# Value products over whole key tiles, flat loads for the bounds, and the softmax constant from a column: one change to an attention and two-layer MLP kernel

## The chip, the cores and the metric

The kernel runs on one core of a Trainium2 chip. The metric is the device time of one execution in microseconds (us); of several executions the median is taken. Beside the time there is one profiled execution, and its span is the time from its first to its last instruction.

The engines are named as the profile names them: PE is TensorE (matmuls), PEld its weight loads, DVE is VectorE, ACT is ScalarE, POOL is GpSimd, and SP issues the DMAs.

## The reference

Causal attention with a decay, then two dense layers. There are 4 batches, 8 heads, 576 positions and 64 columns a head; the inputs are float32.

```python
scores = q @ k^T / 8
cum = cumsum(log(clip(f, 1e-4, 1)))
scores = where(causal, -1e9, scores + cum[:, None] - cum[None, :])
attn = exp(scores - max); attn = attn / (sum(attn) + 1e-9)
x = (attn @ v), heads side by side: 2304 x 512
h = x @ w_in (512 x 2048); x = (h * tanh(softplus(h))) @ w_out (2048 x 512)
h = x @ w2_in (512 x 1024); solu = h * softmax(h)
out = (layer norm of solu * g_ln) @ w2_out (1024 x 512)
```

## The kernel before

**Precision.** PE works on float16. Each float32 operand is split into a high and a low float16 part after a scaling by a power of two, and each product is three matmuls: high by high, high by low, low by high. The scale of k and v of a batch comes from a bound on their size: `stats` (line 290) sums squares along rows on ACT, one column for each chunk, and `scales` (line 314) takes the largest column and sums over the partitions.

**Attention.** A batch is cut into five tiles of key or query rows (`rows_of`, line 75). In batch 0 tile 4 holds only rows 0 to 63; in batches 1 to 3 tile 0 holds only rows 64 to 127, and all others are whole. For each query tile i a slot handles four heads (i = 0), two (i = 1) or one (i of 2 to 4):

- `step_s` makes the scores; the matmuls of line 418 contract 128 rows, those of line 419 contract 67.
- `step_r` (line 452) takes the maximum on DVE and the exponential on ACT. It writes the float32 probabilities into one of two tiles `p32`, which are set to zero once at the start, and the sums of rows into `rsum`.
- `step_h` (line 484) splits them into float16 (`ph`), and one DMA transposes them to `pT`, with the keys on the partitions.
- `step_pv` (line 515) makes the value products, for each head and each key tile c up to i three matmuls of 64 columns (lines 537 to 539). The rows that they contract are the valid rows of key tile c, so they are 64 for the half tile and 128 for every other tile.
- `fin` (line 541), once for each query tile, adds 1e-9 to the sums (line 549; the last tile first adds its two partial sums, line 548), takes the reciprocal, scales the product and transposes it into `xT`, from which the first dense layer reads.

**Loads.** k and v of a batch are read twice: once early for the bounds and once when they are split. `ahead` (line 625) does both for the next batch during query tiles 2 to 4. Both readings use `load_raw` (line 274), which reads 64 float32 of a head at a time, so each packet has 256 bytes. All raw tiles share one rotation of three buffers.

**Dense layers.** `up` (line 764) and `down` (line 808) are the matmuls of the first, with ACT, DVE and POOL between them; `Stage2` (lines 1430 and 1470) is the second, which can start its weights only when attention's memory is free.

**Order.** The class `Order` takes all instructions with their dependences, works out a duration for each, simulates them several times and pins the order of the instructions of every engine that ended earliest. Its duration of a matmul (`weigh`, line 1120) is made from the columns alone:

```python
c = elems(next(b for t, b, w in acc if w)) / 2.4
o.cols += c
o.d += max(c + 2.5, 28.0)
```

The functions that the change touches are these.

Of the kernel before, what the change touches and what calls it, by code (L numbers as in the profile page):

```python
# [9 lines left out]
F32 = mybir.dt.float32  # L10
# [181 lines left out]
def emit(tc, q, k, v, f, w_in, w_out, w2_in, w2_out, g_ln, out):  # L192
# [94 lines left out]
            )  # L287
        return i

    def stats(b, c, which):  # L290

        if ("st", b) not in sc:
            sc["st", b] = att.tile([P, 2, NCH], F32, tag="st", name=f"st_{b}", bufs=2)
            nc.vector.memset(sc["st", b], 0.0)
        r0, r1_, _ = rows_of(b, c)
        for nm in which:
            jk = attd.tile([P, DM], F32, tag="x32", name=f"jk{nm}_{b}_{c}", bufs=1)
            nc.scalar.activation(
                jk[r0:r1_], raw[nm, b, c][r0:r1_], AF.Square,
                accum_out=sc["st", b][r0:r1_, "kv".index(nm), c:c + 1])  # L300
# [64 lines left out]
    def split_v(b, c):  # L365
        r0, r1_, _ = rows_of(b, c)
        vc = attd.tile([P, 2, DM], F16, tag="vt", name=f"vt_{b}_{c}", bufs=6)
        vt[b, c] = vc
        rv = raw["v", b, c][r0:r1_]
        s = sc["v", b][r0:r1_]  # L370
        split(nc, vc[r0:r1_, 0], vc[r0:r1_, 1], rv, s, qmode(b, c, 1))
# [80 lines left out]
    def step_r(b, i, hs):  # L452
        m, off, end, sp, wd = pend.pop(("s", b, i, hs))
        if (b, i) not in pend:
            pend[b, i] = attd.tile([P, 2, H], F32, tag="rsum", name=f"rsum_{b}_{i}", bufs=2)
        rs = pend[b, i]
        ng = len(hs)
        nm = attd.tile([P, 4], F32, tag="nm", name=f"nm_{b}_{i}_{hs[0]}", bufs=2)
        pt = p32[cnt["p32"] % len(p32)]
        cnt["p32"] += 1  # L460
        pv = pt.rearrange("p c s -> p (c s)")
        pend["p", b, i, hs] = (m, pt)
        if i < NCH - 1:
            s3 = sp[:m, :wd * ng].rearrange("p (g s) -> p g s", g=ng)
            nc.vector.tensor_reduce(nm[:m, :ng], s3[:, :, off:end], axis=AX.X, op=ALU.max, negate=True)  # L465
            for g, h in enumerate(hs):
                nc.scalar.activation(  # L467
                    pv[:m, g * (i + 1) * P + off:g * (i + 1) * P + end], s3[:, g, off:end],
                    AF.Exp, bias=nm[:m, g:g + 1], accum_out=rs[:m, 0, h:h + 1])
            return  # L470
        h = hs[0]
        ex = sps[2][:m].rearrange("p (h s) -> p h s", h=H)
        if h == 0:
            ne = attd.tile([P, H], F32, tag="ne", name=f"ne_{b}", bufs=1)
            nc.vector.tensor_reduce(ne[:m], ex, axis=AX.X, op=ALU.max, negate=True)
            pend["ne", b] = ne
        ne = pend["ne", b]
        nc.vector.tensor_reduce(nm[:m, 0:1], sp[:m], axis=AX.X, op=ALU.max, negate=True)
        nc.vector.tensor_tensor(nm[:m, 0:1], nm[:m, 0:1], ne[:m, h:h + 1], op=ALU.min)
        x0, m0 = (off, 128) if off else (512, 0)  # L480
        nc.scalar.activation(pv[:m, x0:x0 + 64], ex[:, h], AF.Exp, bias=nm[:m, 0:1], accum_out=rs[:m, 1, h:h + 1])
        nc.scalar.activation(pv[:m, m0:m0 + 512], sp[:m], AF.Exp, bias=nm[:m, 0:1], accum_out=rs[:m, 0, h:h + 1])  # L482
# [32 lines left out]
    def step_pv(b, i, hs):  # L515
        if len(hs) == 1:
            if hs[0] % 2 == 0:
                return
            hs = (hs[0] - 1, hs[0])
        r0, r1_, _ = rows_of(b, i)  # L520
        m = r1_ - r0
        pT = pend.pop(("pT", b, i, hs[0]))
        if hs[0] == 0:
            if pv0 and i == 1:
                pend["pv", b, i] = pv0.pop().tile([P, DM], F32, tag="x2_0", name=f"pv_{b}_{i}")
            else:
                pend["pv", b, i] = pspv.tile([P, DM], F32, tag="pv", name=f"pv_{b}_{i}")
        acc = pend["pv", b, i]
        for g, h in enumerate(hs):
            o = acc[:m, h * D:(h + 1) * D]  # L530
            for c in range(i + 1):
                a0, a1, _ = rows_of(b, c)
                vc = vt[b, c]
                vh = vc[a0:a1, 0, h * D:(h + 1) * D]
                vl = vc[a0:a1, 1, h * D:(h + 1) * D]
                k = 2 * (g * (i + 1) + c)
                nc.tensor.matmul(o, pT[a0:a1, k, :m], vh, start=(c == 0), stop=False)  # L537
                nc.tensor.matmul(o, pT[a0:a1, k, :m], vl, start=False, stop=False)  # L538
                nc.tensor.matmul(o, pT[a0:a1, k + 1, :m], vh, start=False, stop=(c == i))  # L539

    def fin(b, i):
# [2 lines left out]
        rs = pend.pop((b, i))  # L544
        acc = pend.pop(("pv", b, i))
        rr = attd.tile([P, H], F32, tag="rr", name=f"rr_{b}_{i}", bufs=2)
        if i == NCH - 1:
            nc.vector.tensor_tensor(rs[:m, 0], rs[:m, 0], rs[:m, 1], op=ALU.add)
        nc.vector.tensor_scalar(rr[:m], rs[:m, 0], 1e-9, None, op0=ALU.add)
        nc.vector.reciprocal(rr[:m], rr[:m])  # L550
        x32 = attd.tile([P, DM], F32, tag="x32", name=f"x32_{b}_{i}", bufs=1)
        nc.vector.tensor_tensor(
# [72 lines left out]
    def ahead(b, i, h):  # L625

        nb, ni = (b, i + 1) if i + 1 < NCH else (b + 1, 0)
        if b + 1 < B and i in (2, 3, 4):
            n = (i - 2) * H + h
            if n in (6, 8, 14, 15, 16):  # L630
                load_raw(b + 1, (6, 8, 14, 15, 16).index(n), "kv")
            if n in (8, 10, 15, 16, 17):
                stats(b + 1, (8, 10, 15, 16, 17).index(n), "kv")
            if n == 18:
                scales(b + 1, "kv")
        if nb < B:
            if h == (LD if ni else 3) and nb > 0:
                load_raw(nb, ni, "qkv")
            if h == LD and nb == 0 and ni >= 3:
                load_raw(nb, ni, "q")  # L640
            if h == (LD + 2 if ni else 4):
                if nb or ni > 1:
                    split_k(nb, ni)
                    split_q(nb, ni)
                split_v(nb, ni)
# [307 lines left out]
EARLY = {"PE": 0.0, "ACT": 103.0, "DVE": 79.0, "POOL": 37.0, "SP": -45.0}  # L953
LATE = {"PE": 53.0, "ACT": 34.0, "DVE": 33.0, "POOL": 77.0, "SP": 27.0}
HEAD = 126.0
PERIOD = 3413.33
BACKLOG = 1500.0
LANDED = 600.0
# [20 lines left out]
class Order:  # L979
# [140 lines left out]
    def weigh(self):  # L1120

        for o in self.ops:
            if o.eng == "PE":
                for i, acc in o.ins:
                    c = elems(next(b for t, b, w in acc if w)) / 2.4
                    o.cols += c
                    o.d += max(c + 2.5, 28.0)
                    if size_of(next(t for t, b, w in acc if not w).dtype) == 4:
                        o.d += 200.0
# [72 lines left out]
    def plan(self, rank):  # L1202
# [8 lines left out]
        free["SP"] = free["-"] = 0.0  # L1211
        seq = {e: [] for e in engs}
        state = {"lock": 0.0, "dma": 0.0, "end": 0.0}
        busy, warm, win = {}, False, 0
        self.start = start = [0.0] * len(ops)

        def give(o, t):
# [9 lines left out]
        while todo:  # L1227
# [35 lines left out]
            elif e == "PE":  # L1263
# [5 lines left out]
                while todo_c > 1e-6:  # L1269
# [6 lines left out]
                    if todo_c > 1e-6:  # L1276
                        warm = busy[win] / PERIOD >= (0.38 if warm else 0.85)
                        win += 1
                end = t + o.d + x - t - o.cols
                seen = end + 165  # L1280
            elif o.lock:
                end = seen = max(t + HEAD, state["lock"]) + max(o.d - HEAD, 20.0)
# [239 lines left out]
```

## Time and profile before

| | us |
|---|---|
| median of 3 runs | 811.48 (811.48 to 812.52) |
| the profiled execution | 813.11 |
| its span | 811.3 |

| engine | busy, us | share of the span |
|---|---|---|
| PE | 729.6 | 90% |
| DVE | 603.1 | 74% |
| ACT | 546.6 | 67% |
| POOL | 404.3 | 50% |

The profile shows one execution. Busy times are unions of instruction times; matmuls are pipelined, so the listed time of one matmul is longer than its step, and the step is read from the starts of neighbours in the timeline. A row of the timeline merges neighbours of one kind and gives their start, the time from the first start to the last end, and their count. Idle time of an engine costs something only where that engine sets the end.

### The profile page before, as it was taken

What the parts mean: (1) busy time and instruction counts of PE and PEld (TensorE: products, weight loads), DVE (VectorE), ACT (ScalarE), POOL (GpSimd) and SP (SyncE); (2) the same over time, 40 slices, a digit from 0 to 9 for tenths busy, and PEclk for the clock granted to TensorE, in tenths of its full rate; (3) what the DMA queues carried; (4) which work ended last, traced back from release to release, by engine and by line L of the source; (5) the groups of instructions that cost most, each with busy time, mean ns of one, the idle gap of its engine ahead of it and who ended that gap; (6) DMA issues with size and microseconds to landing.
All of it is one profiled execution on the core that took longest, in us unless ns stands there. A gap on an engine that the chain in (4) does not pass through costs nothing.

```text
span 811.3 us, 15742 instructions
## 1 busy us (share of the span) xinstructions
PE 729.6 (90%) x5822; PEld 457.6 (56%) x5822; DVE 603.1 (74%) x1168; ACT 546.6 (67%) x1201; POOL 404.3 (50%) x321
## 2 busy tenths in 40 slices
PE   0345568799999999999999999999999999999998
PEld 0233336476666767676677767665565554444443
DVE  4799998878788887869988966687877437355651
ACT  4464649968996979798986776798694544233332
POOL 2153246766685775675878773247473312112221
PEclk9975659899999999999999999999999999999999
DMA  8999998778987999877997652732313422534543
GB/s 210 246 246 235 256 201 166 142 130 150 172 148 151 188 155 172 159 148 139 172 187 145 124 111 70 212 142 79 88 44 78 85 59 66 117 78 108 112 87 84
DMA packets 328569, 114.84 MB, mean 142 GB/s; under 512 B 317676, under 2 KB 317676, under 8 KB 328492
## 3 DMA queue, kind: packets, MB, share of 16 engines
q1 hardware_dynamic: 328492, 113.84, 67.0%
q8 instruction: 45, 0.74, 0.4%
q14 instruction: 32, 0.26, 0.1%
HBM read 46.59 MB, written 9.55 MB: 69 GB/s over the span
## 4 chain that ended last, share of the span: by engine, by line
PE 66%; DVE 14%; issue 6%; ACT 5%; DMA 5%; POOL 4%; SPq 1%; POOLq 0%; DVEq 0%; ACTq 0%
PE x L808 17%; PE h L764 17%; PE h L1430 10%; PE o L1470 9%; PE pv L537 4%; PE sp L418 2%; PE sp L419 2%; DMA w2i_r<-in_moe_w_in_dram 2%; PE pv L538 1%; PE pv L539 1%; DVE wout L125 1%; DVE win L182 1%; DMA zT<-z 1%; DVE wout L127 1%; DVE win L125 1%
## 5 line engine op out<-in xcount | busy, mean ns | idle before, releaser
L808 PE MATMUL x<-wout,gt 128*128 128x512 f16 x864 | 217.6, 385 | 1.7 <-POOL gt L791 1.5
L764 PE MATMUL h<-xT,win 128*128 128x256 f16 x1728 | 214.4, 276 | 1.6 <-ACT th L777 0.9
L506 POOL TENSOR_TENSOR ph<-p,ph 128x512 f16<-128x512 f32 (+4 forms) x120 | 158.6, 1328 | 83.4 <-ACT ph L505 47.6
L764 PEld LDWEIGHTS <-win 128*128 128x128 f16 x1728 | 168.3, 99 | 41.6 <-issue 4.0
L791 POOL TENSOR_TENSOR gt<-th,gt 128x512 f16<-128x512 f32 x72 | 93.2, 1296 | 101.6 <-ACT gt L790 99.0
L808 PEld LDWEIGHTS <-gt 128*128 128x128 f16 x864 | 81.0, 99 | 74.4 <-POOL gt L791 4.3
L1458 POOL TENSOR_TENSOR z<-sl,z 128x1024 f16<-128x1024 f32 x18 | 41.3, 2292 | 128.9 <-DVE s2c L1437 62.7
L1430 PE MATMUL h<-w,x2T 128*128 128x512 f16 x432 | 96.2, 379 | 0.0
L1470 PE MATMUL o<-wo,zT 128*128 128x512 f16 x432 | 95.7, 379 | 0.1
L785 DVE SCALAR_TENSOR_TENSOR th<-ta,th 128x512 f32<-128x512 f32 x72 | 67.1, 934 | 27.9 <-ACT ta L784 26.9
L467 ACT ACTIVATE p<-sp,nm 64x64 f32<-64x64 f32 (+7 forms) x128 | 61.3, 485 | 21.7 <-DVE nm L465 13.3
L537 PE MATMUL pv<-vt,pT 128*128 128x64 f16 (+3 forms) x480 | 71.1, 201 | 3.2 <-DMA pT<-ph 3.1
L1470 PEld LDWEIGHTS <-zT 128*128 128x128 f16 x432 | 42.2, 98 | 51.1 <-DMA zT<-z 0.6
L1430 PEld LDWEIGHTS <-x2T 128*128 128x128 f16 x432 | 42.3, 98 | 50.3
L538 PE MATMUL pv<-vt,pT 128*128 128x64 f16 (+3 forms) x480 | 70.0, 196 | 0.0
L539 PE MATMUL pv<-vt,pT 128*128 128x64 f16 (+3 forms) x480 | 70.0, 196 | 0.0
L776 ACT ACTIVATE ta<-h,usc 128x512 f32<-128x512 f32 (+3 forms) x96 | 53.2, 577 | 19.6 <-PE h L764 18.4
L418 PE MATMUL sp<-ktr,qa 128*128 128x64 f16 (+6 forms) x304 | 58.7, 253 | 7.6 <-ACT p L482 3.7
L419 PE MATMUL sp<-ktr,qb 67*128 67x64 f16 (+6 forms) x304 | 62.8, 255 | 2.2 <-DVE qb L383 1.5
L537 PEld LDWEIGHTS <-pT 128*128 128x128 f16 (+3 forms) x480 | 45.3, 101 | 31.6 <-issue 15.8
L781 DVE TENSOR_SCALAR ta<-ta 128x512 f32<-128x512 f32 x72 | 51.8, 723 | 14.0 <-ACT ta L776 13.7
L1441 ACT ACTIVATE e<-h,s2c 128x1024 f32<-128x1024 f32 x18 | 21.7, 1203 | 57.6 <-DVE s2c L1439 53.7
(228 smaller groups left out, 1398.3 us busy)
## 6 DMA issues: line engine op xcount, KB each, us to landing
wi_r<-in_moe_w_in_dram SPq DMA_DIRECT2D x8, 1024.0 KB
wo_r<-in_moe_w_out_dram SPq DMA_DIRECT2D x8, 1024.0 KB
rawk<-in_k_dram SPq DMA_DIRECT2D x25, 256.0 KB
rawv<-in_v_dram SPq DMA_DIRECT2D x25, 256.0 KB
x2d<-x2h SPq DMA_DIRECT2D x18, 256.0 KB
out_dram<-ro SPq DMA_DIRECT2D x18, 256.0 KB
w2i_r<-in_moe_w_in_dram SPq DMA_DIRECT2D x4, 1024.0 KB
w2o_r<-in_moe_w_out_dram SPq DMA_DIRECT2D x4, 1024.0 KB
```

Of the source, the lines that this page charges most:

```text
L418: nc.tensor.matmul(d, qa[:, h, r0:r1_], k1, start=True, stop=False)
L419: nc.tensor.matmul(d, qb_[:67, h, r0:r1_], k2, start=False, stop=not diag)
L506: nc.gpsimd.tensor_tensor(p4[:, :, 1], pv3, p4[:, :, 0], op=ALU.subtract)
L537: nc.tensor.matmul(o, pT[a0:a1, k, :m], vh, start=(c == 0), stop=False)
L538: nc.tensor.matmul(o, pT[a0:a1, k, :m], vl, start=False, stop=False)
L539: nc.tensor.matmul(o, pT[a0:a1, k + 1, :m], vh, start=False, stop=(c == i))
L764: nc.tensor.matmul(ph, win[:, (fi // 4) * NC1 + c, col:col + P], x[:, lx * NC1 + c, :], start=(m == 0), stop=(m == 3 * NC1 - 1))
L785: nc.vector.scalar_tensor_tensor(th, ta, 2.5, th, op0=ALU.subtract, op1=ALU.mult)
L791: nc.gpsimd.tensor_tensor(gt[:, 1], th, gt[:, 0], op=ALU.subtract)
L808: nc.tensor.matmul(o, gt[:, lg, n % 2, t * P:(t + 1) * P], wout[:, fi, lw * 512:(lw + 1) * 512], start=(first and m == 0), stop=(last and ...
L1430: nc.tensor.matmul(h[:, half * 512:(half + 1) * 512], x[:, lx * NC1 + c, :], self.w2[:, half * NC1 + c, lw * 512:(lw + 1) * 512], start=(n ...
L1470: nc.tensor.matmul(o, zT[:, lz * NF2 + c, :], self.wo[:, c, lw * 512:(lw + 1) * 512], start=(n == 0), stop=(n == 3 * NF2 - 1))
```

## The change

There are three parts, and the planner is told of the first.

1. In `step_pv` every query tile but tile 0 contracts all 128 rows of each key tile. For this the unused half of a value tile is set to zero on POOL (`split_v`), and for query tile 1 the unused columns of `p32` are set to zero on POOL in the first two slots of each of batches 1 to 3 (`step_r`).
2. For batches 1 to 3 the early reading of k and v uses `load_flat`: the batch is seen as 128 rows of 2304 numbers, and each of five loads takes 512 of them (the last 256), so that a packet has 2 KB (1 KB).
3. `rsum` gets a third column block that DVE sets to 1e-9, and `fin` makes the sum with one reduction over two blocks. The last query tile adds its two partial sums and no constant.
4. The planner charges 95 ns where a matmul of at most 64 contracted rows follows one of more, or the reverse.

```diff
+    def load_flat(b, c):
+        n = min(DM, H * S * D // P - c * DM)
+        for nm, src in (("k", k), ("v", v)):
+            t = rawp.tile([P, DM], F32, tag="raw", name=f"flat{nm}_{b}_{c}")
+            raw[nm, b, -1 - c] = t[:, :n]
+            nc.sync.dma_start(
+                t[:, :n], src[b].rearrange("h s d -> (h s d)").rearrange("(p x) -> p x", p=P)[:, c * DM:c * DM + n])
+
+    def stats_flat(b, c):
+        stats(b, c, "kv", True)
+
-    def stats(b, c, which):
+    def stats(b, c, which, flat=False):
...
+            if flat:
+                x = raw.pop((nm, b, -1 - c))
+                nc.scalar.activation(
+                    jk[:, :x.shape[-1]], x, AF.Square, accum_out=sc["st", b][:, "kv".index(nm), c:c + 1])
+                continue
...
         vt[b, c] = vc
+        if r0:
+            nc.gpsimd.memset(vc[:r0], 0.0)
+        elif r1_ < P:
+            nc.gpsimd.memset(vc[r1_:], 0.0)
...
-            pend[b, i] = attd.tile([P, 2, H], F32, tag="rsum", name=f"rsum_{b}_{i}", bufs=2)
+            pend[b, i] = attd.tile([P, 3, H], F32, tag="rsum", name=f"rsum_{b}_{i}", bufs=2)
+            nc.vector.memset(pend[b, i][:, 2], 1e-9)
...
+        if off and i == 1 and hs[0] // ng < len(p32):
+            nc.gpsimd.memset(pt[:, 0:2 * ng:2, :off], 0.0)
...
-                a0, a1, _ = rows_of(b, c)
+                a0, a1 = (0, P) if i else rows_of(b, c)[:2]
                 vc = vt[b, c]
...
-        if i == NCH - 1:
-            nc.vector.tensor_tensor(rs[:m, 0], rs[:m, 0], rs[:m, 1], op=ALU.add)
-        nc.vector.tensor_scalar(rr[:m], rs[:m, 0], 1e-9, None, op0=ALU.add)
+        st = 1 if i == NCH - 1 else 2
+        nc.vector.tensor_reduce(
+            rr[:m], rs[:m, 0:3:st].rearrange("p j h -> p h j"), axis=AX.X, op=ALU.add)
         nc.vector.reciprocal(rr[:m], rr[:m])
...
-                load_raw(b + 1, (6, 8, 14, 15, 16).index(n), "kv")
+                load_flat(b + 1, (6, 8, 14, 15, 16).index(n))
...
-                stats(b + 1, (8, 10, 15, 16, 17).index(n), "kv")
+                stats_flat(b + 1, (8, 10, 15, 16, 17).index(n))
...
+SWITCH = 95.0
...
+                o.rows = [next(b for t, b, w in acc if not w).ap[0][1] > 64 for i, acc in o.ins]
+                o.d = SWITCH * sum(a != b for a, b in zip(o.rows, o.rows[1:]))
...
-                end = t + o.d + x - t - o.cols
+                end = o.d + x - o.cols + (SWITCH if o.rows[0] != rows else 0.0)
+                rows = o.rows[-1]
```

## Rows read from the trace of the kernel before

**Rows 1.** The page: busy us (share) and instructions by engine; the chain that ended last.
```profile
PE 729.6 (90%) x5822; PEld 457.6 (56%) x5822; DVE 603.1 (74%) x1168; ACT 546.6 (67%) x1201; POOL 404.3 (50%) x321
PE 66%; DVE 14%; issue 6%; ACT 5%; DMA 5%; POOL 4%; SPq 1%; POOLq 0%; DVEq 0%; ACTq 0%
```

**Rows 2.** Stretches: length; busy us (instructions) of each engine; clock; DMA share; GB/s.
```profile
40.00:120.00 80.00, 43.75 (x349) 29.72 (x349) 78.68 (x135) 43.11 (x84) 31.26 (x19) 0.62 1.01 240
120.00:160.00 40.00, 31.56 (x331) 21.53 (x332) 35.59 (x80) 39.85 (x99) 26.15 (x19) 0.88 0.77 149
160.00:240.00 80.00, 79.56 (x735) 54.21 (x736) 65.19 (x110) 67.60 (x160) 54.38 (x51) 0.97 0.85 153
240.00:501.00 261.00, 261.00 (x2675) 182.29 (x2676) 212.23 (x390) 212.84 (x515) 182.01 (x160) 1.00 0.80 148
501.00:600.00 99.00, 98.70 (x656) 62.92 (x654) 74.70 (x138) 81.68 (x140) 48.49 (x29) 1.00 0.38 117
600.00:811.30 211.30, 207.54 (x1032) 100.59 (x1030) 111.81 (x275) 83.35 (x159) 52.64 (x30) 1.00 0.40 86
```

**Rows 3.** Waits from 160 to 501 us: us in total, times, longest.
```profile
PE h L764 <- ACT th L777: 0.4, 1, 0.4
```

**Rows 4.** Timeline of PE, batch 1: start, us, line, rows*columns of the array, form.
```profile
300.06 1.47 PE L764 MATMUL h<-xT,win 128*128 128x256 f16 x12
301.37 2.75 PE L808 MATMUL x<-wout,gt 128*128 128x512 f16 x12
304.06 0.20 PE L537 MATMUL pv<-vt,pT 64*128 64x64 f16 x1
...
304.25 0.20 PE L537 MATMUL pv<-vt,pT 128*128 128x64 f16 x1
...
304.44 0.20 PE L537 MATMUL pv<-vt,pT 64*128 64x64 f16 x1
```

**Rows 5.** Timeline of PE, batch 0, whole tiles; then scores of 67 rows.
```profile
137.56 0.20 PE L537 MATMUL pv<-vt,pT 128*128 128x64 f16 x1
...
137.74 0.19 PE L537 MATMUL pv<-vt,pT 128*128 128x64 f16 x1
...
169.48 0.19 PE L419 MATMUL sp<-ktr,qb 67*128 67x64 f16 x1
169.51 0.22 PE L418 MATMUL sp<-ktr,qa 128*128 128x128 f16 x1
```

**Rows 6.** Groups by line and form, PE, from 160 to 240 us, then from 240.
```profile
L537 PE MATMUL pv<-vt,pT 64*128 64x64 f16 x17 | 3.4, 199 | 0.0
...
L537 PE MATMUL pv<-vt,pT 64*128 64x64 f16 x79 | 15.8, 200 | 0.0
```

**Rows 7.** Groups on DVE (busy us, mean ns, idle before), then two instructions in time.
```profile
L549 DVE TENSOR_SCALAR rr<-rsum 128x8 f32<-128x8 f32 (+1 forms) x20 | 8.5, 424 | 2.9 <-ACT p L467 2.8
L548 DVE TENSOR_TENSOR rsum<-rsum 128x8 f32<-128x8 f32 (+1 forms) x4 | 3.7, 913 | 0.0
L320 DVE TENSOR_REDUCE sctkv<-st 128x2 f32<-128x10 f32 x3 | 0.5, 156 | 1.1 <-ACT jkv L298 1.1
L294 DVE MEMSET st<- 128x10 f32 x4 | 0.3, 67 | 0.9 <-PEq L1509 0.8
...
491.07 1.40 DVE L549 TENSOR_SCALAR rr<-rsum 128x8 f32<-128x8 f32 x1
491.04 1.40 POOL L506 TENSOR_TENSOR ph<-p,ph 128x640 f16<-128x640 f32 x1 [0.67 <-DVE rsum L548]
```

**Rows 8.** Groups on POOL and PE.
```profile
L264 POOL MEMSET qb<- 32x1024 f16 x2 | 1.9, 946 | 0.1
L808 PE MATMUL x<-wout,gt 128*128 128x512 f16 x864 | 217.6, 385 | 1.7 <-POOL gt L791 1.5
```

**Rows 9.** The page's DMA queue; SP's issues of the k loads, min/median/max ns.
```profile
q1 hardware_dynamic: 328492, 113.84, 67.0%
L284 SPq DMA_DIRECT2D rawk<-in_k_dram x32: 367/570/1315, 1.3 to 426.9; - x32
```

More of the change, by code (lines that the diff above doesn't have):

```diff
@@ L1213, in plan @@
         state = {"lock": 0.0, "dma": 0.0, "end": 0.0}
-        busy, warm, win = {}, False, 0
+        busy, warm, win, rows = {}, False, 0, True
         self.start = start = [0.0] * len(ops)
```

## The prediction

> **What bounds the kernel now.** I read the page first, for the engine with the largest share and for the chain that ended last. PE is busy for 729.6 of 811.3 us and holds 66% of the chain [rows 1]. An average hides stages, so the table of stretches comes next. From 40 to 120 us DVE is the full engine (78.68 of 80 us), from 120 to 160 us ACT is (39.85 of 40) while PE has 8.4 us free, and from 160 us on PE is full to the end: 79.56 of 80, then 261.00 of 261, then 98.70 of 99 us [rows 2]. The waits agree: in the 341 us from 160 to 501, when attention ends, PE waited in view for 0.4 us [rows 3]. So a microsecond of PE work removed between 160 and 501 us should leave the end, unless what feeds PE takes its place; before 160 us it should not.
>
> A full PE is not a PE at its peak, so the timeline has to say what the time holds. In batch 1, query tile 1, the value products of one head are three matmuls of 64 rows and three of 128. A head begins at 304.06 us and the next at 304.44: 0.38 us for six matmuls [rows 4]. In batch 0, where all tiles are whole, six matmuls of the same 64 columns take 137.74 - 137.56 = 0.18 us [rows 5]. The extra 0.20 us sits at the edges. The 128-row matmul at 304.25 starts 0.19 us after the group at 304.06, for three matmuls that elsewhere take 0.09. At the other edge, twelve matmuls of line 764 follow one another into line 808 with no loss (12 steps of 0.109 us = 1.31, and line 808 starts 1.31 us after line 764). The twelve of line 808 have steps of about 0.216 us, so their last ends its step at 303.96; the 64-row matmul starts at 304.06, 0.10 us later [rows 4]. PE thus loses about 0.10 us whenever the contracted rows change between 64 and 128. It loses nothing for 67 rows: a score matmul of 67 rows at 169.48 is followed by one of 128 at 169.51, the 0.03 us of an ordinary step [rows 5].
>
> **Part 1, whole key tiles.** In batches 1 to 3 each of 8 heads has a 64-row group in query tiles 1 to 4: 3 x 4 x 8 = 96 groups, 17 of them seen from 160 to 240 us and 79 after [rows 6]. Batch 0 has 8 more, in its last query tile (key tile 4); going by their place in the timeline four lie before 160 us and four behind. The 24 groups of query tile 0 stay at 64 rows. Removed are 104 x 0.20 = 20.8 us of PE time. The 128-row matmul that replaces a 64-row one costs the same 0.03 us step, so nothing comes back there.
>
> What of it lies on the path: the 79 groups after 240 us give 79 x 0.20 = 15.8 us, and I take all of it, since ACT and DVE are at 212.8 and 212.2 of 261 us there [rows 2]; in 245 us they would be at 87%. The 21 groups from 160 to 240 us are worth 4.2 us. ACT has just left a stretch in which it was full, so I take half, 2.1 us; the bounds are 0 and 4.2. The four before 160 us (0.8 us) are hidden behind ACT: 0. Sum: 15.8 + 2.1 = 17.9 us. What is late next is the dense layer's gt, made on ACT, DVE and POOL: line 808 already waited 1.5 us for POOL's half of it [rows 8].
>
> The order helps. The planner of before makes a matmul's time from its columns, so the order it pinned already supposes a PE without these losses; the real PE ran behind it and its inputs came with slack. That slack goes, but the order need not be found anew.
>
> New work: four memsets of half a value tile, 64 x 1024 float16. The nearest is POOL's memset of 32 x 1024 at 0.946 us [rows 8], so 4 x 0.95 = 3.8 us, and six memsets of 128 numbers a row, each between 0 and that price; I take 0.3 us, so 1.8 us. POOL has 182 of 261 us busy [rows 2], so 5.6 us more in 340 is covered. Queued behind a memset are the low halves of ph and gt; each could come 1 us later, and PE would feel it only where gt is already just in time. If that cover were gone in every case it would cost 5.6 us on the path.
>
> The Trainium skill, "TensorEngine Tiling (Array Packing)", section "Theoretical Speedup", speaks against this part: a contraction of at most 64 rows can gain up to 2x from row tiling, which a padded matmul gives away. By that rule 104 groups would lose half of their 0.09 us, 4.7 us, and the estimate would be 798.3 us. The trace does not bear it out: steps inside a 64-row group are 0.03 us, as in a 128-row one. The same page, section "Key Properties", says that a change of tiling mode drains the engine, and there the trace agrees with 0.10 us.
>
> **Part 2, flat loads.** Each of batches 1 to 3 loses 2 x (4 x 1024 + 512) = 9,216 packets of 256 bytes, 27,648 in all, and gains 3,840 of 2 KB or less; the bytes stay at 7.1 MB. All 328,492 packets took 67.0% of 811.3 us [rows 9], 1.65 ns each of the 16 engines together, so at most 27,648 x 1.65 = 46 us are removed. The added ones take 7.1 MB at the best rate seen, 240 GB/s [rows 2], 29 us. The gain is about 16 us of DMA time, between 0 and 46, in stretches where the share is 0.80 to 0.85. PE does not wait for DMA there [rows 3], so the path gets 0. It is cover: with PE 6% faster the same transfers must fit into 6% less time. On SP an issue of this kind takes 570 ns at the median and 367 at the least [rows 9]; 30 x 0.2 = 6 us of SP's queue come free for the transposes behind them, again not on the path. ACT's squares shrink for six half-length chunks, by less than 2 us in all.
>
> **Part 3, the constant.** The small operations of line 549 take 8.5 us for 20 and those of line 548 3.7 us for 4; the one at 491.07 lasts 1.40 us, exactly beside POOL's operation from 491.04 [rows 7]. So they mostly wait for POOL. A reduction of ten numbers takes 0.156 us and a memset 0.067 [rows 7]; 20 of each are 4.5 us against 12.2. DVE gains 7.7 us if the reduction does not wait, 0 if it does. DVE is not full after 160 us, and before it only three or so of these lie: 0 on the path, at most 1.
>
> **The redrawn order.** Every priority is worked out again, so the first 160 us can move either way. An estimate from the idle PE time from 120 to 160 us (8.4 us): about a third of it, 3 us, either way.
>
> The sum is made against the profiled span: 811.3 - 17.9 = 793.4 us. The profiled execution took 813.11, and the median of the runs, 811.48, lies 0.2 above the span, so 793.6 us is the forecast for the median.
>
> **Rivals.** *The feeders become the bound.* PE's gain after 240 us is half eaten by waits on gt and on exponentials: 17.9 - 7.9 = 10.0 us, 801.5 us. For it: ACT was full from 120 to 160 us and DVE at 81% later has to share with POOL. Against it: only 0.4 us of waits in 341 us. *All of it and the opening too.* The 20.8 us come whole and the redrawn opening gives 3 more: 787.7 us. *The loss is not the rows' change.* Then the time stays at 811.5 us; the 67-row steps and the whole tiles of batch 0 speak against it. *Slower, through the clock.* From 40 to 120 us, with PE busy for 43.75 of 80 us, the granted clock is 0.62 in the mean, so PE spent most of that stretch at the lower of its two levels, 1.2 GHz of 2.4 [rows 2]. If PE now outruns ACT from 160 to 240 us and stops often enough to fall to that level for 60 of the 80 us, it does 30 us less work there: 811.5 - 17.9 + 30 = 823.6 us; above 36 us at the lower level the change would be slower. Against it: from 120 to 160 us PE had 8.4 us free and still held 0.88.
>
> **How the numbers follow.** Forecast (789 to 798): 0.62. Feeders: 0.18. Whole gain and opening: 0.10. No change: 0.04. Slower: 0.06. The range goes from 787.5 (20.8 + 3 us gained) to 801.5 (the feeders' case): it takes the forecast, half of the feeders' case and most of the third, about 0.8. A difference of 0.2%, 1.6 us, is about what can be told from no change: faster 0.90, within it 0.04, slower 0.06.
>
> **What would show it.** Right: the rows of line 537 have the form 64*64 in query tile 0 alone, no 64*128; six value matmuls of a head take 0.18 us in batch 1; attention ends near 483 us and the stretch behind it keeps its length; PE's waits after 160 us stay under 3 us; line 549 falls to about 0.16 us; packets under 512 bytes fall by some 27,600 with no change of PE's waits. Wrong: waits of PE on gt or exponentials of 5 us or more after 160 us; a clock under 0.9 there; or an attention that ends no earlier.

## The result, and the profile after

| | before | after |
|---|---|---|
| median, us | 811.48 (810.04 to 812.52, 4 runs) | 800.84 (798.72 to 802.49, 4 runs) |
| the profiled execution | 813.11 | 802.49 |
| its span | 811.3 | 800.7 |
| ratio of the times | | 0.9865 [0.9844, 0.9886] |

The kernel is 10.6 us faster, where 17.9 us had been forecast. 800.84 lies inside the range, but not in the forecast's own 789 to 798: it stands at the range's end, next to the rival "the feeders become the bound" (801.5).

The parts did what they say. The first fence holds the forms of the value matmuls of line 537, now line 561 (line, rows*columns of the array, shape, count, then busy us and mean ns, then the idle time before them), and the second, from the timeline of PE, the first matmuls of three consecutive groups of three in batch 1.

```profile
L561 PE MATMUL pv<-vt,pT 128*128 128x64 f16 x416 | 46.5, 197 | 4.6 <-DMA pT<-ph 4.5
L561 PE MATMUL pv<-vt,pT 128*64 128x64 f16 x40 | 5.1, 210 | 1.2 <-DMA pT<-ph 1.2
L561 PE MATMUL pv<-vt,pT 64*64 64x64 f16 x24 | 3.0, 198 | 0.0
```

```profile
201.47 0.19 PE L561 MATMUL pv<-vt,pT 128*128 128x64 f16 x1
201.56 0.19 PE L561 MATMUL pv<-vt,pT 128*128 128x64 f16 x1
201.64 0.19 PE L561 MATMUL pv<-vt,pT 128*128 128x64 f16 x1
```

The 64*128 form of [rows 6] is gone and 64*64 is left 24 times. Six matmuls take 201.64 - 201.47 = 0.17 us, against the 0.38 of [rows 4]. The page's row of busy times, and then the stretches of [rows 2] (length; busy us and instructions of PE, PEld, DVE, ACT and POOL; clock; DMA share; GB/s):

```profile
PE 706.5 (88%) x5822; PEld 450.9 (56%) x5822; DVE 603.9 (75%) x1184; ACT 541.6 (68%) x1201; POOL 406.5 (51%) x331
```

```profile
120.00:160.00 40.00, 36.05 (x354) 24.99 (x354) 34.02 (x79) 39.13 (x90) 22.05 (x16) 0.92 0.64 115
160.00:240.00 80.00, 73.41 (x770) 51.13 (x767) 67.98 (x115) 69.62 (x171) 59.15 (x55) 0.98 0.82 156
240.00:501.00 261.00, 251.50 (x2709) 182.14 (x2707) 214.85 (x409) 215.93 (x528) 188.74 (x169) 1.00 0.83 154
501.00:600.00 99.00, 99.00 (x640) 62.33 (x638) 86.05 (x146) 83.30 (x143) 50.65 (x32) 1.00 0.39 114
600.00:800.70 200.70, 196.91 (x965) 94.17 (x963) 99.93 (x256) 73.24 (x143) 42.18 (x24) 1.00 0.41 88
```

With these rows the account can be made. PE is busy for 729.6 - 706.5 = 23.1 us less [rows 1], against the 20.8 us worked out for the row changes; the 2.3 us between them are not explained, and the mean clock of the first 160 us differs in the two executions (0.78 and 0.94). PE is idle for 94.2 us instead of 81.7: 12.5 us more. The difference, 10.6 us, is what the span lost. The idle time is new in one place only: from 160 to 501 us PE was free for 0.4 us in 341, and now for 6.6 + 9.5 = 16.1. Before 160 and behind 501 us it is a little less than it was. What PE waited for in those 341 us (us in total, times, longest):

```profile
PE pv L561 <- DMA pT<-ph: 5.7, 6, 1.5
PE h L788 <- ACT th L801: 3.0, 1, 3.0
PE sp L440 <- DVE qb L404: 2.2, 1, 2.2
PE sp L439 <- ACT p L506: 1.6, 3, 1.0
PE x L832 <- POOL gt L815: 1.5, 2, 0.8
PE sp L439 <- ACT p L491: 1.1, 1, 1.1
...
```

With two smaller ones, of 0.8 us together, they are 15.9 us in 16 waits, on transposes, ACT, DVE and POOL alike, where [rows 3] had one of 0.4 us. The stretch behind 240 us cut finer, first of the kernel before, then of the one after:

```profile
240.00:380.00 140.00, 140.00 (x1428) 97.14 (x1429) 112.20 (x215) 117.59 (x291) 95.81 (x85) 1.00 0.86 159
380.00:430.00 50.00, 50.00 (x522) 35.34 (x520) 45.10 (x85) 43.69 (x112) 38.80 (x34) 1.00 0.93 171
430.00:490.00 60.00, 60.00 (x621) 41.79 (x619) 47.76 (x76) 44.97 (x103) 44.48 (x41) 1.00 0.61 117
```

```profile
240.00:380.00 140.00, 133.10 (x1450) 96.26 (x1448) 124.70 (x239) 120.57 (x304) 103.80 (x93) 1.00 0.92 174
380.00:430.00 50.00, 47.40 (x535) 34.58 (x534) 44.22 (x81) 42.68 (x111) 39.28 (x38) 1.00 0.96 171
430.00:490.00 60.00, 60.00 (x622) 43.34 (x620) 40.91 (x79) 44.58 (x101) 41.33 (x37) 1.00 0.59 107
```

From 240 to 380 us DVE rose from 112.2 to 124.7 of 140 us (89%) and the DMA share from 0.86 to 0.92, and PE is free for 6.9 us. From 430 us on PE is full as before. From 380 to 430 us the chain of what released what reads, by line, first before, then after:

```profile
by line: PE h L764 39.1%; PE x L808 33.9%; PE pv L537 9.7%; PE sp L418 4.6%; PE sp L419 4.2%; PE pv L539 3.2%; PE pv L538 3.2%; PE sp L423 2.4%
```

```profile
by line: DMA pT<-ph 31.1%; issue 10.7%; POOL ph L530 9.9%; PE h L788 5.2%; POOL gt L815 3.9%; ACT p L491 3.9%; DVE th L809 3.9%; DVE ph L527 3.8%; PE x L832 3.5%; DVE ktr L376 2.9%; POOL kn L189 2.7%; ACT gt L814 2.0%; PE sp L439 1.8%; POOL
```

Before, PE follows PE. After, the chain runs through the exponential, the split on DVE and POOL and the transposition, and PE is a small part of it. The transpositions are the largest: three of them, at 381.13, 411.57 and 419.64 us, take 6.70, 3.85 and 5.01 us from issue to landing, with the DMA share at 0.96. The chain of the kernel after can be followed back to 370 us only, so it says nothing of the waits before that.

The smaller edits (groups on DVE and POOL; then the page's rows on the DMA queue and the packets):

```profile
L572 DVE TENSOR_REDUCE rr<-rsum 128x8 f32<-128x16 f32 (+3 forms) x20 | 3.3, 167 | 4.9 <-ACT p L491 4.5
L477 DVE MEMSET rsum<- 128x8 f32 x20 | 1.3, 65 | 0.0
L387 POOL MEMSET vt<- 64x1024 f16 x3 | 2.8, 947 | 0.1
L486 POOL MEMSET p<- 128x128 f32 x6 | 1.6, 261 | 0.3
```

```profile
q1 hardware_dynamic: 304684, 113.84, 67.4%
DMA packets 304761, 114.84 MB, mean 143 GB/s; under 512 B 290028, under 2 KB 290796, under 8 KB 304684
```

### The profile page after: what moved, and what is told of

The parts are those of the page before. It is cut to its first block, busy times and chain, and to the rows that moved or that the text cites. A ratio compares the mean times of both kernels' runs of the same rounds, so it can differ in the third digit from the quotient of the medians.

```text
span 800.7 us, 15754 instructions
## 1 busy us (share of the span) xinstructions
PE 706.5 (88%) x5822; PEld 450.9 (56%) x5822; DVE 603.9 (75%) x1184; ACT 541.6 (68%) x1201; POOL 406.5 (51%) x331
## 2 busy tenths in 40 slices
DMA packets 304761, 114.84 MB, mean 143 GB/s; under 512 B 290028, under 2 KB 290796, under 8 KB 304684
## 3 DMA queue, kind: packets, MB, share of 16 engines
q1 hardware_dynamic: 304684, 113.84, 67.4%
## 4 chain that ended last, share of the span: by engine, by line
PE 43%; DMA 3%; POOL 2%; DVE 2%; issue 2%; ACT 1%; POOLq 0%; DVEq 0%; ACTq 0%
PE x L832 11%; PE h L1458 11%; PE h L788 10%; PE o L1498 9%; DMA pT<-ph 2%; DMA zT<-z 1%; POOL ph L530 1%; PE sp L439 0%; PE sp L440 0%; PE pv L561 0%; PE pv L562 0%; PE pv L563 0%; DVE ph L527 0%; POOLq L1546 0%; POOL z L1486 0%
## 5 line engine op out<-in xcount | busy, mean ns | idle before, releaser
L832 PE MATMUL x<-wout,gt 128*128 128x512 f16 x864 | 214.9, 381 | 5.1 <-ACT gt L814 2.6
L1486 POOL TENSOR_TENSOR z<-sl,z 128x1024 f16<-128x1024 f32 x18 | 38.3, 2128 | 120.6 <-DVE s2c L1465 65.9
L805 DVE TENSOR_SCALAR ta<-ta 128x512 f32<-128x512 f32 x72 | 47.9, 666 | 16.7 <-ACT ta L800 16.6
L561 PE MATMUL pv<-vt,pT 128*128 128x64 f16 (+2 forms) x480 | 54.6, 198 | 5.8 <-DMA pT<-ph 5.7
L814 ACT CAST gt<-th 128x512 f16<-128x512 f32 x72 | 44.5, 617 | 18.4 <-DVE th L809 15.8
L561 PEld LDWEIGHTS <-pT 128*128 128x128 f16 (+2 forms) x480 | 46.1, 103 | 16.1 <-DMA pT<-ph 7.6
L562 PE MATMUL pv<-vt,pT 128*128 128x64 f16 (+2 forms) x480 | 54.3, 198 | 0.0
```

Of the source, the lines that this page charges most:

```text
L832: nc.tensor.matmul(o, gt[:, lg, n % 2, t * P:(t + 1) * P], wout[:, fi, lw * 512:(lw + 1) * 512], start=(first and m == 0), stop=(last and ...
```

## The experiments

Two theories stood against each other first. In the first, the row changes cost what was worked out, PE gave the time back whole, and something beside them took 7 us: the redrawn order, the flat loads or the constant. In the second, PE and what feeds it were nearly level before, and with PE faster the feeders set the time. Ratios are against the kernel before, run beside each experiment on the same chip, with 95% intervals; the medians of that kernel were 811.95, 812.01, 812.15 and 811.76 us in the four comparisons.

### Each part alone, and the rows with the order held

**Row changes with the order of before.** Only part 1 is taken. The planner is given a price of zero for the ten memsets, so that every engine keeps its order of before but for the memsets on POOL and one exchanged pair on ACT.

```diff
-                a0, a1, _ = rows_of(b, c)
+                a0, a1 = (0, P) if i else rows_of(b, c)[:2]
...
+        if eng == "POOL" and kind == "InstMemset" and acc[-1][0].name.startswith(("vt_", "p32_")) and n != 640: return 0.0, False
```

> Part 1 alone on the kernel before, and the planner is told that the ten new memsets cost nothing, so that every engine keeps the order of before (no difference on PE, DVE and SP, one swapped pair on ACT, ten memsets put in on POOL). PE loses its 20 us of changes between 64 and 128 rows. Theory 'order' (the redrawn order of the changed kernel costs what is missing): 791 to 796 us, and PE's waits after 160 us stay under 5 us. Theory 'feeders' (ACT, DVE, POOL and the transposes cannot feed a PE that is 6% faster, in any order): 799 to 803 us, with 10 us or more of new waits of PE after 160 us. Theory 'other parts' (the flat loads or the constant cost what is missing): 791 to 796 us.

Measured: 804.27 us, 0.9917 [0.989, 0.9944], a little above the range of the theory "feeders" and far from the other two. The stretch from 160 to 501 us of the kernel before, then of this one, and this one's waits of PE there:

```profile
160.00:501.00 341.00, 340.56 (x3407) 236.50 (x3408) 277.42 (x499) 280.44 (x674) 236.40 (x210) 0.99 0.81 149
```

```profile
160.00:501.00 341.00, 331.44 (x3521) 238.61 (x3519) 287.43 (x511) 290.35 (x696) 247.25 (x223) 1.00 0.82 153
```

```profile
PE pv L537 <- DMA pT<-ph: 2.9, 4, 1.6
PE sp L418 <- ACT p L482: 2.6, 3, 1.3
...
```

With the order held, no flat loads and no constant, PE is again free for 9.6 us and the kernel gains 7.7 us. So the missing gain needs none of the other parts and no new order. The kernel after is some 4 us faster than this one (0.9865 against 0.9917, and the intervals lie apart); no run separates which of the new order, the planner's 95 ns and the other parts brings that.

**Row changes with the order redrawn.** The same edit, with the planner pricing the memsets as it does, but without its 95 ns for a change of rows.

> Part 1 alone on the kernel before, the order drawn anew with the memsets at their price. Theory 'order': another time than with the order of before by 3 us or more, since it is another draw, between 792 and 804 us. Theory 'feeders': 799 to 803 us, as with the order of before. Theory 'other parts': 791 to 796 us.

Measured: 803.34 us, 0.9896 [0.9864, 0.9927]. The interval holds the kernel after as well as the one above; redrawing makes no difference that can be told.

**Flat loads alone.** Part 2 on the kernel before.

```diff
-                load_raw(b + 1, (6, 8, 14, 15, 16).index(n), "kv")
+                load_flat(b + 1, (6, 8, 14, 15, 16).index(n))
```

> Part 2 alone on the kernel before (flat loads for the bounds), the order drawn anew, PE keeps its losses. Theory 'other parts': 814 to 820 us, with new waits of PE for transposes. Theory 'feeders': within 2 us of the kernel before, since PE is slow enough to be fed. Theory 'order': 808 to 816 us, either way.

Measured: 811.17 us, 0.999 [0.9972, 1.0007]: no difference.

**The constant alone.** Part 3 on the kernel before.

```diff
-        nc.vector.tensor_scalar(rr[:m], rs[:m, 0], 1e-9, None, op0=ALU.add)
+        nc.vector.tensor_reduce(
+            rr[:m], rs[:m, 0:3:st].rearrange("p j h -> p h j"), axis=AX.X, op=ALU.add)
```

> Part 3 alone on the kernel before (the constant from a column), the order drawn anew, PE keeps its losses. Theory 'other parts': 813 to 818 us. Theory 'feeders': within 2 us of the kernel before. Theory 'order': 808 to 816 us, either way. In each the reduction takes about 0.16 us in place of 0.42, if it does not wait for POOL.

Measured: 817.91 us, 1.0076 [1.005, 1.0102]: slower by 6.0 us. From 160 to 501 us:

```profile
160.00:501.00 341.00, 332.25 (x3335) 228.74 (x3334) 271.26 (x502) 279.44 (x675) 239.74 (x211) 0.98 0.82 151
```

```profile
PE sp L419 <- DVE qb L383: 4.6, 2, 3.8
```

DVE has less to do, but PE is free for 8.8 us, and 4.6 us of its waits are for a copy of query rows (`qb`) that DVE made late. The operation that was made cheaper is not in that wait. The order was redrawn here too, so an unlucky draw would explain it and the reduction itself need not.

**The whole change without the constant.**

> The changed kernel without its part 3 (1e-9 is added by the small operation of before). With all three parts it takes 800.8 us; part 3 alone on the kernel before took 817.9 against 812.0. If the constant from a column costs by itself: 795 us or less. If what it cost there was the draw of an order: 799 to 804 us, like every draw with whole key tiles (800.8, 803.3, 804.3).

Measured: 801.64 us (800.11 to 805.77), 0.9855 [0.9819, 0.9891], against 0.9865 with it. So in the changed kernel the constant costs nothing that can be told. That the 6 us of the run above are the draw is argued from these two runs; no run held the order and changed the constant alone, so it is not shown.

### Relieving one feeder at a time

In the next four the kernel after keeps its order, and one feeder is given less to do; each leaves out the part of the computation that its edit names. If one engine or queue set the time, its relief would bring the missing 7 us.

**Thinner early loads.** Each flat load brings 64 of its 512 columns.

```diff
-                t[:, :n], src[b].rearrange("h s d -> (h s d)").rearrange("(p x) -> p x", p=P)[:, c * DM:c * DM + n])
+                t[:, :64], src[b].rearrange("h s d -> (h s d)").rearrange("(p x) -> p x", p=P)[:, c * DM:c * DM + 64])
```

> The changed kernel with its order held on every engine; each early load brings only 64 of its 512 columns, and the square reads these eight times, so ACT's time is kept and the transfer nearly vanishes (left out: seven eighths of what the bounds of batches 1 to 3 are made from). The changed kernel takes 800.8 us, with PE free for 16 us from 160 to 501 us. Theory 'transfers' (late transposes are what PE now waits for): 793 to 797 us, with half or more of the 16 us gone. Theory 'engines' (ACT, DVE or POOL feed PE late): 799 to 801 us. Theory 'hand-over' (each step of the chain waits for the one before, no engine or queue is full): 798 to 801 us.

Measured: 801.14 us, 0.9864 [0.9849, 0.9879]. The DMA share from 160 to 501 us falls from 0.83 to 0.78 and PE is free for 15.7 us instead of 16.1: no gain. From 380 to 430 us, where the transpositions are the longest part of the chain, the run did not relieve the queue (0.95 against 0.96):

```profile
380.00:430.00 50.00, 46.79 (x528) 34.30 (x526) 43.91 (x79) 42.63 (x110) 38.31 (x38) 1.00 0.95 169
```

So the early loads are not what PE waits for; that the queue holds it there is not ruled out.

**Less for ACT.** The squares of the bounds read 64 columns, and one of ACT's six passes between `up` and `down` covers half of its tile.

```diff
-                    jk[:, :x.shape[-1]], x, AF.Square, accum_out=sc["st", b][:, "kv".index(nm), c:c + 1])
+                    jk[:, :64], x[:, :64], AF.Square, accum_out=sc["st", b][:, "kv".index(nm), c:c + 1])
...
-        nc.scalar.activation(ta, ta, AF.Square)
+        nc.scalar.activation(ta[:, 0], ta[:, 0], AF.Square)
```

> The changed kernel with its order held; ACT does less: the squares for the bounds take 64 of 512 columns, and the square inside the dense layer's activation (line 806) takes one of the two column blocks (left out: seven eighths of the bounds' sample, and that square for half the hidden units). ACT loses 72 x 0.26 + 30 x 0.4 = about 31 us, some 20 of them before 501 us. Theory 'engines', if ACT is the one: 792 to 796 us. If DVE or POOL is the one, or by 'transfers': 799 to 801 us. 'Hand-over': 797 to 800 us, as the chain of an activation gets 0.26 us shorter.

Measured: 804.89 us, 0.9908 [0.9892, 0.9925]. ACT has 12.4 us less to do from 160 to 501 us, PE is free for 13.7 us instead of 16.1, and the time is no better; it is about 4 us worse than that of the kernel after, with the same order, and outside every range named. PE was busy for 83.92 of the first 160 us here, against 85.65 after. Why ACT's relief costs time there is open.

**Less for DVE.** The clamp of line 805 and the last product of line 809 cover half of their tiles.

```diff
-        nc.vector.tensor_scalar(ta, ta, E20, 1.0, op0=ALU.min, op1=ALU.add)
+        nc.vector.tensor_scalar(ta[:, 0], ta[:, 0], E20, 1.0, op0=ALU.min, op1=ALU.add)
...
-        nc.vector.scalar_tensor_tensor(th, ta, 2.5, th, op0=ALU.subtract, op1=ALU.mult)
+        nc.vector.scalar_tensor_tensor(th[:, 0], ta[:, 0], 2.5, th[:, 0], op0=ALU.subtract, op1=ALU.mult)
```

> The changed kernel with its order held; DVE does less: the clamp (line 805) and the last product (line 809) of the dense layer's activation take one of the two column blocks (left out: both for half the hidden units). DVE loses 72 x (0.14 + 0.27) = 30 us at least, some 18 of them before 501 us, and more where it waited with POOL. Theory 'engines', if DVE is the one: 792 to 796 us. If ACT is the one, or by 'transfers': 799 to 801 us. 'Hand-over': 797 to 800 us.

Measured: 797.27 us, 0.9811 [0.9788, 0.9835]. From 160 to 501 us:

```profile
160.00:501.00 341.00, 329.41 (x3508) 236.60 (x3507) 260.34 (x525) 288.85 (x703) 238.20 (x223) 0.99 0.85 160
```

DVE has 22.5 us less to do and PE is free for 11.6 us instead of 16.1; the kernel gains 3.6 us on the one after, half of the missing gain. POOL is busy for 238.20 us here against 247.9 after, so the run does not relieve DVE alone. ACT's relief moved the time by 4 us the other way, so that DVE is a part of the bound is likely and not shown. The time lies in the range of "hand-over", just above that of "engines".

**All three at once.**

> The changed kernel with its order held and all three reliefs together: thin early loads, less work on ACT, less on DVE (left out: what the three leave out). Whatever feeds PE late is now earlier: 788 to 793 us by each theory, with less than 5 us of PE free from 160 to 501 us. If it stays above 797 us, what holds PE is none of these three: POOL, or PE's own order of waits.

Measured: 798.12 us, 0.9817 [0.9789, 0.9845], 5 us above the range; PE is free for 11.3 us. Relieving loads and ACT on top of DVE brings nothing, and the gain with DVE is there again. So neither DVE, nor ACT, nor the early loads set the time alone or together. The relief of POOL and that of the transpositions weren't tried.

### What the planner supposes

**A later landing.** The planner takes a DMA's result as usable 600 ns after its transfer; here it takes 1500, and the order is redrawn.

```diff
-LANDED = 600.0
+LANDED = 1500.0
```

> The changed kernel with one number of its planner altered: it counts 1.5 us, not 0.6, from the end of a DMA's data until its reader may start. All work is the same; the order is drawn anew with transposes and loads that arrive 0.9 us later in the plan. Theory 'optimistic plan' (PE's order reaches value products before their transposes have landed, always in the same places): 794 to 798 us, with PE's waits on transposes from 160 to 501 us under 2 us (5.7 in the changed kernel). Theory 'hand-over' (any order hands the time back elsewhere): 799 to 803 us, with PE free for 14 us or more in that stretch.

Measured: 805.77 us, 0.9913 [0.9885, 0.9941]. PE's waits from 160 to 501 us:

```profile
PE pv L561 <- DMA pT<-ph: 0.5, 1, 0.5
PE sp L439 <- ACT p L505: 3.7, 1, 3.7
PE sp L439 <- ACT p L506: 3.5, 5, 0.9
...
```

The waits on transposes fall from 5.7 to 0.5 us and others take their place; PE is free for 13.9 us, and the time lies above both ranges, 5 us behind the kernel after. The same work in another order can thus cost 5 us. The largest wait of a list is not the cause of the sum.

**Slower feeders in the plan.** The planner prices ACT, DVE and POOL 6% longer, and the landing at 1200 ns.

```diff
+                o.d *= 1.06
...
-LANDED = 600.0
+LANDED = 1200.0
```

> The changed kernel whose planner counts 6% more for every instruction of ACT, DVE and POOL, and 1.2 us in place of 0.6 for a landing. All work is the same. 'Optimistic plan': 792 to 797 us, with under 8 us of PE free from 160 to 501 us, since PE is then given work that is ready. 'Hand-over': 799 to 803 us, 14 us or more free.

Measured: 799.24 us (798.96 to 799.69), 0.9832 [0.9806, 0.9858]. PE is free for 9.7 us, and the last group of value matmuls starts at 484.0 us, against 492.3 in the kernel after. Yet the time is that of the kernel after, within the intervals: the dense work that the order had not done by then is done later. By its free time of PE the run fits neither theory, by its time "hand-over".

### Taking more work from PE

The last run asks whether PE sets the time at all. In the kernel after, with its order held, the low part of the first dense product covers 128 of its 256 columns, so part of that product is left out: one of every three matmuls of line 788 is half as wide.

```diff
-                    ph, win[:, (fi // 4) * NC1 + c, col:col + P], x[:, lx * NC1 + c, :],
+                    ph[:, :P] if lx else ph, win[:, (fi // 4) * NC1 + c, col:col + P], x[:, lx * NC1 + c, :P] if lx else x[:, lx * NC1 + c, :],
```

> The changed kernel with its order held on every engine, and less work on PE alone: in the first dense layer the product with the low half of x takes 128 of 256 columns (left out: that correction for half of the tokens). These 576 matmuls get 0.053 us shorter each: 168 thirds before 160 us, 352 of them from 160 us to attention's end at 493 us (18.8 us), 168 behind it (9.0 us). If PE is still what sets the end of attention, 771 to 777 us, with 18 us gone before attention ends. If attention's end is set by those who feed PE (theories 'engines' and 'hand-over'): 786 to 792 us, since only the 9 us behind attention and less than a quarter of the 18.8 count. In between, each microsecond of PE work gives half a microsecond, as part 1 did: 780 to 785 us.

Measured: 798.44 us, 0.9817 [0.9786, 0.9848]. The page's row of busy times, forms of line 788, two groups in the timeline, the stretches from 160 to 501 us and from there to 600, and the longest waits of PE in the first:

```profile
PE 687.8 (86%) x5822; PEld 429.0 (54%) x5822; DVE 599.0 (75%) x1184; ACT 541.5 (68%) x1201; POOL 405.6 (51%) x331
```

```profile
L788 PE MATMUL h<-xT,win 128*128 128x256 f16 x1152 | 175.1, 277 | 5.8 <-ACT th L801 5.5 <-DMA xT<-xh 0.2
L788 PE MATMUL h<-xT,win 128*128 128x128 f16 x576 | 56.6, 222 | 0.0
```

```profile
609.27 1.26 PE L788 MATMUL h<-xT,win 128*128 128x256 f16 x12
610.36 1.46 PE L832 MATMUL x<-wout,gt 128*128 128x512 f16 x6
```

```profile
160.00:501.00 341.00, 313.01 (x3476) 219.23 (x3474) 274.43 (x522) 286.59 (x699) 246.83 (x222) 0.98 0.84 155
501.00:600.00 99.00, 94.13 (x621) 56.58 (x619) 89.56 (x145) 81.51 (x139) 51.41 (x33) 0.97 0.37 112
```

```profile
PE pv L561 <- DMA pT<-ph: 12.8, 11, 2.7
PE sp L439 <- ACT p L506: 5.0, 8, 1.4
...
```

Twelve matmuls of line 788 with four narrow ones take 610.36 - 609.27 = 1.09 us, against the 1.31 us from 300.06 to 301.37 in [rows 4]. 1728/12 = 144 such groups are about 31 us of PE's steps (576 narrow matmuls at 0.053 us are 30.5), some 20 of them from 160 to 501 us (1095 of the 1728 matmuls). The time fell by 2.4 us, from 800.84 to 798.44, hardly more than the intervals can tell, and none of the three ranges holds it. PE's free time there rose from 16.1 to 28.0 us, and the waits on transposes from 5.7 to 12.8. Not even the 9 us behind attention came: from 501 to 600 us PE is busy for 94.13 us, where it was full in the kernel after. In the order that the change pinned, PE does not set the time any more up to 600 us; only behind that is it busy almost throughout (196.91 of 200.70 us after). An order drawn for the narrower product might use more of it; that wasn't tried.

## Why the prediction was right and wrong

**Right: the price and the place of the row changes.** 0.20 us for a 64-row group was read from neighbours in [rows 4] and [rows 5]; the pairs, then 0.38 us, take 0.17 now, and PE is busy for 23.1 us less against 20.8 worked out. The rival "the loss is not the rows' change" is out. A whole 128-row matmul costs no more than a 64-row one. The Trainium skill, "TensorEngine Tiling (Array Packing)", section "Theoretical Speedup", lets a contraction of at most 64 rows gain up to 2x from row tiling. The steps of 0.03 us in 64-row groups before and in 128-row ones after show nothing of such a gain to lose here.

**Wrong: "I take all of it".** The step that failed is the 15.8 us of the 79 groups after 240 us, taken whole because ACT and DVE stood at 212 of 261 us and "in 245 us they would be at 87%". An average of 87% over 261 us was read as room. It hid stretches such as 380 to 430 us, where before the change DVE was at 90% (45.10 of 50 us) and the DMA queue at 0.93, and it says nothing of how the engines hand work to one another: a tile of scores goes from PE to DVE for its maximum, to ACT for the exponential, to ACT, DVE and POOL for the split and through a transposition back to PE. These times add up though no engine is full, as the chain from 380 to 430 us shows for that stretch; for the rest it is argued. PE is now free for 9.5 us from 240 to 501 us. The rival had put 7.9 us there. An estimate that prices every matmul at the step its neighbours show (0.03 us for 64 columns, 0.109 for 256, 0.216 for 512, others between) gives PE 246 us of work in that stretch now, against 241 before: some 5 of the 15.8 us came there.

**Wrong: "only 0.4 us of waits in 341 us" as evidence.** It was held against the feeders' case. A wait shows that an input came late; no wait shows only that it came in time, not by how much. The run that left out a further 31 us for a gain of 2.4 shows how little was left. The right question was how long each input had lain ready before PE took it; whether the trace of before would have shown it is open.

**Wrong: PE's waits after 160 us "stay under 3 us".** They are 15.9 us in the list above. The sign named for "wrong", waits on gt or exponentials of 5 us or more, did not quite come (ACT's exponentials 2.7 us and gt 1.7), while the longest item is the transposes, which the prediction had not named; what is late next is not one thing.

**The opening** was taken at 0, with 3 us either way. In the two profiled executions it gave more. The matmuls of the dense layer in the first 160 us, two rows before and two after:

```profile
L764 PE MATMUL h<-xT,win 128*128 128x256 f16 x120 | 17.2, 303 | 1.2 <-DMA xT<-xh 0.7 <-ACT th L777 0.5
L808 PE MATMUL x<-wout,gt 128*128 128x512 f16 x18 | 8.4, 601 | 1.4 <-POOL gt L791 1.3
```

```profile
L788 PE MATMUL h<-xT,win 128*128 128x256 f16 x168 | 23.0, 294 | 0.7 <-DMA xT<-xh 0.5 <-ACT th L801 0.2
L832 PE MATMUL x<-wout,gt 128*128 128x512 f16 x39 | 11.2, 422 | 2.9 <-ACT gt L814 2.4 <-POOL gt L815 0.5
```

The 48 and 21 more are 48 x 0.109 + 21 x 0.216 = 9.8 us of steps; some 2 us of attention's matmuls come later in exchange. By the estimate above PE is thus 7.5 us of work ahead of the kernel before at 160 us, 5.5 us at 240 and 10.3 us at 501. From 160 to 501 us, where some 20 us of row changes went, it won about 3 us. The run with the order of before has no such lead (47.1 us of work at 160 us, against 47.9 before) and is 10.1 us ahead at 501 us all the same. So in these two runs the feeders let PE get about 10 us ahead by the end of attention, with a lead from the opening or without it. The agreement of the sum with the measured time is in part luck: the lead was not forecast, and the row changes gave less than they were priced at.

**From 160 to 240 us** I took half of 4.2 us. PE is free for 6.6 us there now, and its lead fell from 7.5 to 5.5 us, so nothing of these 2.1 us shows.

**The end of attention** was forecast near 483 us and came at 492.3, by the start of the last group of value matmuls. As a sign it was poor: with slower feeders in the plan it is 484.0 and the total is still 799.24, and with the flat loads alone it is 495.8 against the 501.2 of before with no gain at all. The order moves dense work across that line.

**Flat loads: 0 on the path was right, the DMA gain was not.** 317,676 packets below 512 bytes became 290,028, which is 27,648 fewer, as worked out. But the queue's time went from 67.0% of 811.3 = 543.6 us to 67.4% of 800.7 = 539.7: 4 us, where 16 were estimated. Summed by size in the traces, the packets of 256 bytes took 434.5 us of the 16 engines together before (308,608 of them, 22.5 ns each on one engine) and 407.0 after (280,960 of 23.2 ns): 27.5 us went, not 46. The packets of 1 and 2 KB that came took 23.7 us, against the 29 estimated. The term priced the removed packets at the mean of all, 1.65 ns, in which those of 4 KB (197 ns on one engine, so 12.3) weigh too; a 256-byte packet took 1.4. The rest is either removed packets cheaper than their kind's mean or others that now take longer, which the runs don't separate. Thinner loads gave nothing either, so the path got what was forecast.

**The constant** fell to 0.167 us (0.16 forecast), and the memsets cost 65 ns (67). On DVE this is 4.6 us against the 12.2 of [rows 7], though DVE's busy time as a whole did not fall (603.9 us against 603.1); on the path nothing can be told. **The memsets on POOL** took 0.947 us (0.95 forecast) and 0.261 us (0.3).

**The clock** stayed at 0.98 to 1.00 after 160 us in spite of PE's 16 us of idle time, so the slower rival did not come.

**What stays open:** which hand-over in the loop from scores to value product sets the pace. DVE seems to have a share, 3.6 us when it is relieved of 22.5. The early loads and ACT have none that shows. POOL, and the transpositions with the queue that carries them, weren't tried.

## What to carry to other kernels

A microsecond taken from a full engine is worth a microsecond only up to the slack of its inputs. An engine at 100% without waits doesn't show that slack, and neither does a mean of 82% on its feeders: look at how long the inputs lie ready, and at the fullest stretch, before taking such a gain whole. Compare how much work an engine has done by a given time, not only how long it was busy: it shows where a gain is made and where it is handed back. To find whether an engine still sets the time, take more work from it with the order held; that one run told more here than the relief of any feeder.

## What the runs showed of the hardware

DMA time did not follow the count of packets. 27,648 packets of 256 bytes, replaced by 3,840 of 2 KB or less with the same bytes, took 4 us off the queue's 544. In the trace of the kernel after, a packet of 256 bytes takes 23.2 ns in the mean, one of 2 KB 98.6 and one of 4 KB 197: eight times the bytes for four times the time, and from 2 KB on in proportion.

A change between 64 and 128 contracted rows cost PE about 0.10 us each way, and a change between 67 and 128 nothing that shows ([rows 4], [rows 5]). With the changes gone, six value matmuls went from 0.38 to 0.17 us.

PE's busy time hides short stalls. Leaving out some 31 us of steps lowered it by 706.5 - 687.8 = 18.7 us only (the page's rows of the kernel after and of the one with the narrower product). A small matmul is listed with some 0.20 us where its step is 0.03 [rows 5], so a stall shorter than the rest counts as busy. The starts of neighbours bear this out: after 160 us, steps that are over 20 ns too long without listed idle time (changes of rows left out) are 101 in the kernel after, 8.0 us together, and 177 in the run with the narrower product, 18.7 us. PE's free time in the tables here is thus a lower bound.
